# One token load in place of two, key weights in two loads instead of four, and a new order of all work, in a fused attention and GLU kernel

## The chip, the cores and the metric

The kernel runs on one core of one Trainium2 chip. The metric is the device time in microseconds (us). A core has five engines that run at the same time and each work through their own instructions in order: TensorE (PE, matrix products into PSUM), VectorE (DVE), ScalarE (ACT), GpSimd (POOL) and SyncE (SP, which only issues transfers here). They wait for one another through semaphores. Transfers (DMA) are issued by SP or ACT into that engine's own queue and are moved by 16 DMA engines.

## What is computed

Two blocks get the same input x (2048 tokens of 512 values, bf16), and a gate per token mixes them. The other input B_x isn't used.

```python
x = A_x
g = _sigmoid((x * gate_w).sum(-1, keepdims=True))
a = _A_ref(x, A_wq, A_wk, A_wv, A_wo, A_beta)
b = _B_ref(x, B_w_gate, B_w_up, B_w_down)
return g * a + (1 - g) * b
```

Block A is attention with a memory. There are 32 heads of 16 values. The tokens are cut into four segments of 512. Within a segment the attention is causal softmax attention; a matrix M and a vector z per head carry what earlier segments held, and a second result is read from them with q after phi(t) = t + 1 for positive t and exp(t) otherwise. A sigmoid of beta mixes both results per head, and wo projects them. Block B is a gated linear unit: (gelu(x w_gate) * (x w_up)) w_down, with 1792 columns in the middle.

## The kernel before, in words

Everything is held with the contracted axis on the partitions. xT is x transposed, 512 tokens at a time, as four blocks of 128 input columns. For each segment s the kernel makes K, Q and V (`project`, tasks K, Q, V), the scores, exponentials, masks and products with V (`attend`: tasks st, exp, msk, pv), the turns of the results (tp, pvp, ot), the memory's read (nz, nd, ndp) and write (mz, mzacc, zq), the gate and up products of the GLU (G, U, with gelu or gd for the gelu and h for the product), and the outputs (out, wo, with wev and oev for the copies and dma for the store).

A task is one step on one engine, such as four matmuls or one copy. Task names carry the segment, a number, and a letter a or b where a product is made in two halves: U0_4b is the second half of the up product of segment 0, column tile 4. A dense half is two matmuls of 512 columns (line 444), a piece of the output is two or three (line 700), a projection wo is four (line 717). The score group st is four or eight small matmuls (line 595) into one large PSUM area X; exp reads the whole of X on ACT (line 601), and the next st can't begin before that. Other products use four PSUM banks, in turn: whoever takes a bank waits until the copy that reads its former content is done.

**The order is written out.** The string `ORDER` at the end of the file lists every task once. `Sched.schedule` walks it and gives each engine its tasks in that order; each engine then works strictly in its order. A word's digit after the colon is the PSUM bank (or the buffer) that the task takes; the letter is the engine where a task has a choice: `a` is ACT and `d` is DVE. So `xev0_1:d` is a copy made by DVE. `Emitter.plan` adds the waits: a task waits for the writers of what it reads and for the readers of what it overwrites.

**The start.** `ld_w` (line 329) issues a plain load, as task ld_ followed by its name. The first segment's x isn't transposed by the transfer, as that of later segments is (`ld_xt`, line 333), but on PE: four pieces of 128 tokens are loaded as rows into a free buffer (x0_0 to x0_3, 128 KB each), PE transposes them against an identity matrix (`turn_x0`, xtr0_0 to xtr0_3, line 772, four transposes each), and DVE copies each result into xT (xev0_0 to xev0_3, line 780). The key weights come as four blocks of 128 rows (wk0 to wk3, 128 KB each). x0_0, x0_2, wk0, wk2 are in this order in SP's queue, x0_1, x0_3, wk1, wk3 in ACT's; wq (two loads), wv, beta and the gate weights follow in SP's. Two tasks wake0 and wake1 (line 366) multiply constants before anything has arrived.

The first segment's K is made in a special way. K0_k0 to K0_k3 (line 466) each take one block i of the key weights and of xT, and add its share for the first 256 tokens to all four banks; K0_ki needs x pieces 0 and 1 and key block i. K0_0b to K0_3b (line 472) make the other 256 tokens. Kev copies a bank to kT (line 436 on ACT, 437 on DVE), kpada and kpadb make the padded keys on DVE (line 483) that the scores need. Q0 and V0 follow.

**The end.** The last outputs' copies (oev, line 721, DVE) and stores (line 726) follow the last wo matmuls, whose 512 columns are made in two halves for the last two token tiles.

Of the kernel before, what the change touches and what calls it, by code (L numbers as in the profile page):

```python
# [235 lines left out]
def _build(es, nc, A_x, A_wq, A_wk, A_wv, A_wo, A_beta, B_w_gate, B_w_up, B_w_down, gate_w, out):  # L236
# [91 lines left out]
    def ld_w(name, eng, dst, src, writes, size, wait=()):  # L328
        load(name, eng, lambda e: e.dma_start(dst, src), writes, size=size, wait=[("ld", w) for w in wait])
# [544 lines left out]
out0_1_0:2 exp1_0D Kev2_3:d Q2_3b Kev2_0:d out0_1_1 Qev2_3:d out0_1_2 st1_0E:0 out0_1_3 kpadb2_3 exp1_0E pvp0_31
msk1_0B ktr1_2 go0 V2_3a:3 vsh1_01 vsh1_00 V2_3b phqc1_0 ktr1_0 ld_wo20 out0_3_0:0 ot0_2 st1_0C:0 out0_1_4 out0_3_1
Vev2_3:a wev0_1:d phka2_0 exp1_0C G1_11a:3 msk1_0E G1_11b kpadb2_0 K2_2a:1 st1_1A:0 out0_0_0:2 K2_2b out0_0_1 out0_0_2
vsh1_20 ot0_3 gd1_11 phqc1_2 Kev2_2:d msk1_0C out0_0_3 msk1_0D vsh1_21 gelu1 wo0_1_0:1 out0_0_4 ktr1_3 wev0_0:d
out0_3_2 out0_3_3 msk1_0A out0_3_4 oev0_1_0 pv1_0:31 exp1_1A wev0_3:a tp1_d00:1 tp1_d01:2 st1_1B:0 ld_x3_2 wo0_0_0:2
# [5 lines left out]
G2_5a:0 G2_5b Gev2_5:a ndp1_0 tp1_d10:1 G2_0b kpada2_3 G2_3b Gev2_0:d st1_2C:0 gate1:0 exp1_2C msk1_2C kpada2_0
Gev2_3:d mz1 G2_1a:2 G2_1b msk1_2B G2_12a:3 mzacc1 st1_2D:0 G2_12b phkb2_2 gz1 Gev2_1:d kpadb2_1 G2_6a:0 dma0_0 G2_6b
G2_9a:1 pvp1_11 exp1_2D Gev2_6:d wo0_2_0:2 G2_9b gd2_9 G2_8a:0 G2_8b oev0_2_0 ndp1_1 wo0_3_0:2 gd2_12 msk1_2D gd2_8
U1_7a:1 U1_7b gelu2 U1_0a:0 phkc2_0 U1_0b G2_13a:3 G2_13b h1_7 oev0_3_0 pvp1_10 U1_3a:1 gd2_13 h1_0 U1_3b h1_3
st1_2E:0 Q2_0a:2 kpadb2_2 exp1_2E U2_5a:3 U2_5b phqa2_2 Q2_0b ot1_0 V2_0a:1 U1_8a:0 h2_5 V2_0b Vev2_0:d phqb2_2
msk1_2E Qev2_0:d st1_3A:0 U1_5a:3 exp1_3A U1_8b U1_5b h1_8 pv1_2:12 st1_3B:0 tp1_d20:2 K3_1a:0 K3_1b exp1_3B h1_5
U1_1a:1 tp1_d21:1 U1_13a:3 U1_13b pvp1_20 pvp1_21 Kev3_1:a st1_3C:0 ktr2_0 U1_11a:2 K3_0a:0 U1_1b U1_11b exp1_3C zq1  # L890
h1_1 h1_11 K3_0b st1_3D:0 V2_2a:1 h1_13 exp1_3D dma2_0 U1_4a:2 V2_2b Q3_0a:3 U1_4b st2_0A:0 ot1_1 Vev2_2:d h1_4
Kev3_0:d Q3_0b msk1_3B ktr2_1 V2_1a:1 msk1_3C exp2_0A msk1_3A Qev3_0:d msk1_3D V2_1b msk2_0A pv1_3:02 st2_0B:0
# [64 lines left out]
```

## Time and profile before

| what | value |
|---|---|
| median of 3 runs | 266.27 us (266.22 to 266.43) |
| the profiled execution | 265.91 us |
| its span, first to last instruction | 264.2 us |
| matmuls | 2829 |
| DMA queues: packets, share of the 16 engines | SP's queue 23454, 22.1%; ACT's queue 720, 0.7% |
| read from HBM, written | 8.14 MB, 2.10 MB |

The profile is one execution, and its times count from the start of the span. A row of an engine's timeline gives the start, the length and the count of like instructions; in brackets stands how long the engine had been idle and who ended that. Matmuls are pipelined: a 512-column one is shown as 380 ns long, though the next starts earlier, so rows of PE overlap and busy time is not a measure of pace. The chain that ended last is followed back from the last instruction: at each step to what released it, or to the instruction before it on its engine. A granted clock of 1.0 is shown for PE.

### The profile page before, as it was taken

Reading aid. Unit: us, or ns where it says so; the run is one execution under the profiler, and the core shown is the slowest. Engines: PE = TensorE matmul, PEld = TensorE weight load, DVE = VectorE, ACT = ScalarE, POOL = GpSimd, SP = SyncE. Lnnn points to the kernel's source line nnn. Section 1 sums busy time; section 2 is a strip of 40 time slices with the busy share of each in tenths; the row PEclk is TensorE's granted clock in tenths of the full one; section 3 lists DMA queues with packets and bytes.
Section 4 is the critical chain, followed back from the end, with each engine's and each line's share of the span. In section 5 each row is a group of like instructions: output and inputs, shape, how many; then the busy total and the mean of one; then the engine's idle time right before and its main releaser. Section 6 shows DMA issues by size and latency. Waiting matters only on the chain.

```text
span 264.2 us, 6633 instructions
## 1 busy us (share of the span) xinstructions
PE 259.8 (98%) x2829; PEld 113.0 (43%) x2829; DVE 203.0 (77%) x381; ACT 205.8 (78%) x166; POOL 97.6 (37%) x159
## 2 busy tenths in 40 slices
PE   8999999999999999999999999999999999999996
PEld 5633434443344443454434343434344443434443
DVE  2678544698989539989788889889986798977864
ACT  1688899989988998999878887569879967376612
POOL 6017333054434635060273535344525035144500
PEclk9999999999999999999999999999999999999999
DMA  6966169930013230002002000010101000000102
GB/s 205 359 115 180 38 77 209 212 116 2 0 42 78 61 82 0 2 4 60 2 0 65 0 2 2 20 42 11 42 14 43 2 2 0 22 20 2 40 2 79
DMA packets 24203, 14.92 MB, mean 56 GB/s; under 512 B 14574, under 2 KB 23150, under 8 KB 24174
## 3 DMA queue, kind: packets, MB, share of 16 engines
q1 hardware_dynamic: 23454, 13.91, 22.1%
q10 hardware_dynamic: 720, 0.59, 0.7%
q8 instruction: 22, 0.36, 0.6%
q14 instruction: 7, 0.06, 0.1%
HBM read 8.14 MB, written 2.10 MB: 39 GB/s over the span
## 4 chain that ended last, share of the span: by engine, by line
PE 92%; DVE 5%; DMA 1%; issue 1%; SPq 0%
PE psD L444 51%; PE psD L700 17%; PE psX L595 9%; PE psD L638 7%; PE psD L717 5%; DMA wk<-in_A_wk_dram 1%; DVE tT L514 1%; DVE phq L457 1%; DVE gb L687 1%; PE psD L466 1%; PE psD L472 1%; DVE kD L483 1%; PE psX L539 0%; PE psD L563 0%; PE psD L529 0%
## 5 line engine op out<-in xcount | busy, mean ns | idle before, releaser
L601 ACT ACTIVATE pt<-psX 128x2048 bf16<-128x2048 f32 x72 | 135.1, 1877 | 34.1 <-PE psX L595 33.9
L607 POOL TENSOR_TENSOR pt<-pt,ctri 128x256 bf16<-128x256 bf16 x128 | 92.4, 730 | 149.5 <-ACT pt L601 132.4
L444 PE MATMUL psD<-xT,wu 128*128 128x512 bf16 x224 | 56.1, 380 | 0.0
L700 PE MATMUL psD<-wd,gb 128*128 128x512 bf16 x224 | 55.1, 380 | 0.0
L444 PE MATMUL psD<-xT,wg 128*128 128x512 bf16 x224 | 54.6, 380 | 0.3 <-DVE gb L687 0.3
L687 DVE TENSOR_TENSOR gb<-psD,gb 128x512 bf16<-128x512 f32 x56 | 37.5, 683 | 10.1 <-PE psD L444 9.9
L514 DVE STREAM_TRANSPOSE tT<-psD 128x512 f32<-128x512 f32 x35 | 23.8, 701 | 13.3 <-PE psD L638 12.8
L444 PEld LDWEIGHTS psD<-xT,wg 128*128 128x128 bf16 x224 | 20.4, 98 | 26.9 <-issue 2.6
L700 PEld LDWEIGHTS psD<-wd,gb 128*128 128x128 bf16 x224 | 20.2, 98 | 26.0 <-issue 3.7
L444 PEld LDWEIGHTS psD<-xT,wu 128*128 128x128 bf16 x224 | 20.0, 98 | 26.1 <-issue 3.5
L595 PE MATMUL psX<-qT,kD 32*128 32x192 bf16 (+7 forms) x512 | 28.5, 287 | 0.2 <-DVE tT L514 0.2
L595 PEld LDWEIGHTS psX<-qT,kD 32*128 32x128 bf16 x512 | 8.2, 92 | 24.6 <-ACT pt L601 19.0
L638 PE MATMUL psD<-pt,vnat 64*17 64x128 bf16 (+7 forms) x512 | 18.7, 283 | 0.0
L649 DVE SCALAR_TENSOR_TENSOR ob<-tT,gq,rc 128x256 bf16<-128x256 f32 x32 | 17.5, 546 | 1.1
L638 PE MATMUL psD<-pt,vsh 64*17 64x128 bf16 (+7 forms) x512 | 18.3, 283 | 0.0
L444 PE MATMUL psD<-wv,xT 128*128 128x512 bf16 x64 | 17.5, 380 | 0.0
L444 PE MATMUL psD<-xT,wq 128*128 128x512 bf16 x64 | 16.6, 380 | 0.0
L437 DVE CAST gb<-psD 128x512 bf16<-128x512 f32 x20 | 13.6, 682 | 3.9 <-PE psD L444 3.8
L717 PE MATMUL psD<-wo,oT 128*128 128x512 bf16 (+1 forms) x72 | 16.2, 356 | 0.0
L678 ACT ACTIVATE gb<-psD 128x512 bf16<-128x512 f32 x28 | 15.0, 603 | 0.6 <-PE psD L444 0.5
L638 PEld LDWEIGHTS psD<-pt,vnat 64*17 64x17 bf16 x512 | 11.6, 86 | 9.1 <-issue 4.7
L721 DVE SCALAR_TENSOR_TENSOR ost<-psD,gtok,wds 128x512 bf16<-128x512 f32 (+1 forms) x18 | 12.2, 685 | 2.9 <-PE psD L717 2.7
(94 smaller groups left out, 250.6 us busy)
## 6 DMA issues: line engine op xcount, KB each, us to landing
out_dram<-ost SPq DMA_DIRECT2D x15, 128.0 KB, 1.7
wg<-in_B_w_gate_dram SPq DMA_DIRECT2D x2, 896.0 KB, 4.8
wu<-in_B_w_up_dram SPq DMA_DIRECT2D x2, 896.0 KB, 5.4
wd<-in_B_w_down_dram SPq DMA_DIRECT2D x2, 896.0 KB, 8.7
vsh<-vnat SPq DMA_DIRECT2D x16, 68.0 KB, 2.1
wq<-in_A_wq_dram SPq DMA_DIRECT2D x2, 256.0 KB, 4.8
wv<-in_A_wv_dram SPq DMA_DIRECT2D x1, 512.0 KB, 5.4
pt<-in_A_x_dram SPq DMA_DIRECT2D x2, 128.0 KB, 2.5
```

The costliest lines, as they stand in the source:

```text
L437: (DVE, 0.60, [I(lambda e: e.tensor_copy(dst, src()), [bk(sl), *reads], writes)]),
L444: one(f"{name}{'abcd'[h // 2]}", PE, 2 * T_MM, [I(lambda e, i=i: e.matmul(BK[sl.i][:, :], lhs(i), rhs(i), start=(i == 0), stop=(i == n - 1 ...
L514: one(f"tp{name}", DVE, 0.605, [I(lambda e, ts=ts, bank=bank: e.transpose(tT[ts.i][:, :], bank()), [key], [("tT", ts)])])
L595: ins.append(I(lambda e, c=c, kb=kb, ncol=ncol, c0=c0, g=g: e.matmul(XALL[:, g * 512 + c0:g * 512 + c0 + ncol], kD[b][quad(g), c, kb, :], ...
L601: one(f"exp{s}_{name}", ACT, 2048 * 0.000833 + 0.05, [I(lambda e: e.activation(pt[slot][:, :, :], xin, ACTF.Exp, scale=ATT_SCALE), [("X", ...
L607: ins.append(I(lambda e, mv=mv: e.tensor_tensor(mv, mv, cm, ALU.mult), [("pt", slot), ("causal",)], [("pt", slot)]))
L638: ins.append(I(lambda e, kb=kb, slot=slot, c0=c0, n=n, g=g, c=c, r0=r0, sl=banks[j], va=va: e.matmul(BK[sl.i][32 * c:32 * c + 17, 64 * kb: ...
L649: I(lambda e, ts=ts, t=t, j=j, dst=dst: e.scalar_tensor_tensor(out=dst, in0=t_rows(ts, 16), scalar=gq[:, 2 * t + j:2 * t + j + 1], in1=rc_ ...
L678: one(f"gd{s}_{ft}", ACT, 0.485, [I(lambda e, gi=gi, f=f, sl=sl: e.activation(gb[gi][:, f, :], BK[sl.i][:, :], ACTF.Gelu_apprx_tanh), [bk( ...
L687: one(f"h{s}_{ft}", DVE, 0.605, [I(lambda e, sl=sl, gi=gi, f=f: e.tensor_tensor(gb[gi][:, f, :], BK[sl.i][:, :], gb[gi][:, f, :], ALU.mult ...
L700: mm.append(I(lambda e, fb=fb, gi=gi, f=f, q=q, sl=sl: e.matmul(BK[sl.i][:, :], gb[gi][:, f, q], wd[:, fb, :], start=(fb == 0), stop=(fb = ...
L717: one(f"wo{s}_{qt}_{ci}", PE, 4 * T_MM / len(parts), [I(lambda e, kb=kb, q=q, so=so, c=c: e.matmul(BK[so.i][:, c], oT[:, kb, q], wo[:, kb, ...
```

## The change

The last two pieces of x0 become one transfer of 256 KB, x0_2, second in SP's queue; pieces 0 and 1 stay as they are, first in SP's and in ACT's. The key weights become two transfers of 256 KB: wk0 (blocks 0 and 1) second in ACT's queue, wk1 (blocks 2 and 3) third in SP's. What is computed is the same, and so are the buffers. The order of all tasks, the banks and the choice of ACT or DVE for copies are new throughout: two of the four xT copies go to ACT, four more of the scaled copies wev and two more of the copies of gate products.

```diff
-    for q in range(4):
-        ld_w(f"x0_{q}", (SP, ACT)[q % 2], pt[stage[0]][:, q, :], A_x[0, 128 * q:128 * q + 128, :], [("xs", q)], 0.125)
-    for i in range(4):
-        ld_w(f"wk{i}", (SP, ACT)[i % 2], wk[:, i, :], wsrc(A_wk)[:, i, :], [("wk", i)], 0.125)
+    for q, (eng, n) in enumerate(((SP, 1), (ACT, 1), (SP, 2))):
+        ld_w(f"x0_{q}", eng, pt[stage[0]][:, q:q + n, :],
+             A_x[0, 128 * q:128 * (q + n), :].rearrange("(q p) d -> p q d", p=P), [("xs", q + j) for j in range(n)],
+             0.125 * n)
+    for h, eng in enumerate((ACT, SP)):
+        ld_w(f"wk{h}", eng, wk[:, halves[h], :], wsrc(A_wk)[:, halves[h], :], [("wk", 2 * h), ("wk", 2 * h + 1)], 0.25)
```

Of the order, the stretches that the text speaks of. The start:

```diff
-wake0:0 masks causal0 ld_x0_1 ld_x0_0 ld_x0_2 ident xtr0_1 vones0 ld_wk0 ld_x0_3 ld_wk2 wake1 ld_wk1 xtr0_0:0 ld_wq0
-ld_wq1 ld_wk3 xtr0_3 xev0_0:d ld_wv xev0_1:d ld_beta xtr0_2 ld_wg0 K0_k0:2031 xev0_2:d K0_k1 K0_k2 ld_wg1 xev0_3:d
-K0_k3 ld_x1_2 K0_1b Kev0_1:a ld_x1_1 kpada0_1 K0_2b kpadb0_1 K0_0b K0_3b Kev0_2:a Kev0_0:a Kev0_3:d Q0_1a:0 Q0_2a:3
+ld_x0_0 wake0:0 wake1 ld_x0_1 ld_wk0 ident xtr0_0:2 ld_x0_2 ld_wk1 masks ld_wq0 vones0 xev0_0:d xtr0_1 xtr0_3 xtr0_2
+xev0_1:a ld_wq1 K0_k0:3021 ld_wv K0_k1 ld_beta ld_wg0 xev0_3:d xev0_2:a ld_wg1 K0_k2 ld_x1_2 K0_k3 ld_x1_1 K0_3b K0_0b
...
+causal0 Q0_2b Qev0_2:a kpada0_2 Q0_0b kpadb0_0 kpada0_1 phka0_2 Q0_3b Qev0_3:a kpadb0_2 Q0_1a:0 kpadb0_1 Q0_1b
+Qev0_0:d V0_1a:2 V0_3a:1 kpada0_0 causal phkb0_2 Qev0_1:d st0_0A:0 V0_0a:0 phkc0_2 V0_3b G0_3a:3 Vev0_3:d V0_0b V0_1b
```

Around the first memory write:

```diff
-U0_4b phqa1_0 ld_x2_0 phkb1_2 h0_8 st0_2C:0 exp0_2C U0_9a:2 pvp0_11 U0_9b h0_4 gate0:3 msk0_2C h0_9 h0_11 mz0 st0_2D:0
-gz0 mzacc0 kpada1_1 ot0_0 U0_5a:1 U0_5b exp0_2D U0_7a:0 U0_1a:2 kpada1_2 U0_7b st0_2E:0 V1_2a:3 V1_2b h0_7 exp0_2E
-G1_5a:0 ld_x2_3 G1_5b msk0_2B U0_1b Gev1_5:a kpadb1_0 h0_5 st0_3A:0 exp0_3A h0_1 U0_6a:1 U0_6b Vev1_2:d U0_12a:0
+U0_4a:3 st0_2C:0 U0_11a:1 U0_11b Qev1_0:a gate0:0 exp0_2C phka1_0 h0_11 ld_wo21 mz0 st0_2D:0 gz0 U0_4b G1_5a:1 V1_2a:2
+G1_5b exp0_2D V1_2b msk0_2C phka1_2 mzacc0 st0_2E:0 U0_7a:0 Gev1_5:a U0_5a:1 h0_4 U0_1a:3 msk0_2A Vev1_2:d msk0_2D
```

Around gelu2, beside the scores of segment 1 (new order alone), and around the memory read of segment 2:

```diff
+st1_2D:0 msk1_2B Gev2_3:d Gev2_0:d phkb2_2 G2_6b G2_8a:1 wo0_2_0:2 G2_12a:3 exp1_2D Gev2_6:d G2_12b gd2_12 G2_9a:0
+G2_8b zq1 G2_9b oev0_2_0 U1_7a:2 gd2_8 gd2_9 U1_8a:3 phkc2_2 G2_13a:1 U1_7b U1_8b phkc2_0 h1_7 G2_13b wo0_3_0:0
+pvp1_11 msk1_2D oev0_3_0 msk1_2C U1_0a:2 st1_2E:0 U1_0b gelu2 gd2_13 U2_5a:1 Q2_0a:0 U2_5b h1_0 h1_8 exp1_2E V2_0a:2
+Q2_0b kpada2_2 Qev2_0:a U1_3a:3 kpadb2_2 h2_5 pvp1_10 U1_3b msk1_2E st1_3A:0 V2_0b h1_3 U1_5a:1 U1_5b Vev2_0:d
...
-kpadb3_0 pv2_0:20 Vev3_1:a st2_1B:0 h1_10 exp2_1B tp2_d00:2 U1_12a:1 tp2_d01:1 U1_12b out1_0_0:3 out1_0_1 phqc2_2
-phqc2_0 st2_1C:0 V3_3a:0 msk2_1B Q3_2a:2 h1_12 out1_0_2 V3_3b exp2_1C ot1_2 nz2:1 tp2_z:0 st2_1D:0 Q3_2b out1_0_3
+K3_3a:3 out1_0_0:1 K3_3b tp2_d01:2 pvp1_20 phqb2_2 exp2_1B out1_0_1 Kev3_3:a st2_1C:0 tp2_d00:1 msk2_1B U1_12a:0
+out1_0_2 exp2_1C ot1_2 ktr2_2 U1_12b V3_3a:3 V3_3b phqc2_2 st2_1D:0 Q3_2a:2 h1_12 msk2_1C exp2_1D pvp2_00 Q3_2b
+out1_0_3 out1_0_4 Qev3_2:a msk2_1D kpadb3_0 st2_2A:0 nz2:0 exp2_2A wev1_0:d tp2_z:0 Vev3_3:a kpadb3_3 wo1_0_0:2
+oev1_0_0 pv2_1:01 st2_2B:0 out1_1_0:3 out1_1_1 out1_1_2 exp2_2B nzp2 dma3_0 V3_2a:2 st2_2C:0 out1_1_3 exp2_2C go1
...
-wo1_1_0:0 exp2_2C pvp2_10 tp2_d11:1 pvp2_11 V3_2a:3 dma4_0 out1_1_3 nd2:0 nzp2 tp2_m1:0 tp2_m0:1 out1_2_1 out1_1_4
-ndp2_1 V3_2b tp2_m3:2 tp2_m2:0 out1_2_2 Vev3_2:a msk2_2C out1_2_3 wev1_1:a out1_3_0:3 msk2_2B phqa3_2 st2_2D:0 exp2_2D
+pvp2_01 tp2_d11:2 out1_1_4 tp2_d10:1 msk2_2B pvp2_11 pvp2_10 wo1_1_0:1 ktr2_0 nd2:0 V3_2b wev1_1:a out1_3_0:3 Vev3_2:a
+out1_2_0:0 tp2_m0:1 tp2_m3:2 ndp2_0 tp2_m1:0 tp2_m2:1 out1_2_1 msk2_2C out1_3_1 out1_3_2 st2_2D:0 out1_2_2 exp2_2D
```

The end:

```diff
-tp3_d30:2 pvp3_31 out3_1_3 pvp3_30 out3_1_4 out3_2_4 wev3_1:a out3_3_0:1 out3_3_1 ot3_3 wo3_0_0:0 wo3_1_0:3 dma10_0
-oev3_0_0 wev3_2:a out3_3_2 out3_3_3 out3_3_4 dma12_0 oev3_1_0 wo3_2_1:0 wo3_2_0:2 oev3_2_1 oev3_2_0 wo3_3_0:3 wev3_3:a
-dma13_0 dma14_1 oev3_3_0 wo3_3_1:1 oev3_3_1 dma15_0 dma15_1
+out3_2_4 wev3_1:a dma11_0 pvp3_31 out3_3_0:1 pvp3_30 ot3_3 out3_3_1 wo3_0_0:0 oev3_0_0 dma12_0 wo3_1_0:3 out3_3_2
+out3_3_3 out3_3_4 oev3_1_0 wo3_2_1:0 wo3_2_0:3 wev3_2:a wo3_3_0:2 oev3_2_1 oev3_2_0 wo3_3_1:0 wev3_3:a dma13_0
+oev3_3_0 dma14_1 dma15_0 oev3_3_1 dma15_1
```

More of the change, by code (lines that the diff above doesn't have):

```diff
@@ L874 @@
[L874 to L878, printed above, removed]
@@ L884 @@
[L884 to L888, printed above, removed]
@@ L889 @@
[L889 to L892, printed above, removed]
-Vev2_1:a U2_6a:1 tp1_d31:2 U2_6b tp1_d30:1 U1_9a:2 U2_13a:3 h2_6 U1_9b vsh2_01 exp2_0B phqa2_0 msk2_0B st2_0C:0
@@ new lines @@
+out0_1_2 V2_3b phqb1_0 out0_3_1 st1_0C:0 out0_3_2 Vev2_3:d zq0 go0 out0_1_3 msk1_0E G1_11b ot0_2 out0_1_4 exp1_0C
+K2_3a:1 K2_3b wev0_1:d ot0_3 gd1_11 st1_1A:0 out0_0_0:2 msk1_0A wo0_1_0:0 Kev2_3:d out0_3_3 out0_0_1 kpada2_1 phqc1_0
+gelu1 vsh1_20 ktr1_3 vsh1_21 out0_0_2 msk1_0C exp1_1A oev0_1_0 out0_3_4 phka2_0 wev0_3:a ld_x3_2 K2_2a:0 K2_2b
+out0_0_3 out0_0_4 Kev2_2:d pv1_0:10 phka2_2 st1_1B:0 wev0_0:d tp1_d00:1 wo0_0_0:3 exp1_1B Q2_1a:2 Q2_1b Q2_2a:1
+oev0_0_0 st1_1C:0 exp1_1C nz1:3 tp1_d01:0 Qev2_1:d msk1_1C out0_2_0:0 msk1_1B out0_2_1 Q2_2b msk1_1A out0_2_2 st1_1D:0
```

106 lines of the change are left out of this document (55 added, 51 removed).

## The prediction

> **What bounds the kernel now.** I read the page first, then the chain that ended last in order of time, and then only the places where TensorE (PE) was late. The engine table comes first, then pieces of the chain (start, length, what):
>
> ```profile
> span 264.2 us, 6633 instructions
> ...
> PE 259.8 (98%) x2829; PEld 113.0 (43%) x2829; DVE 203.0 (77%) x381; ACT 205.8 (78%) x166; POOL 97.6 (37%) x159
> ```
>
> ```profile
> 1.71 3.77 DMA wk<-in_A_wk_dram
> ...
> 5.62 1.95 PE psD L466 x16
> 7.57 1.75 PE psD L472 x16
> 9.31 4.32 PE psD L444 x20
> ...
> 13.96 2.27 PE psD L444 x10
> 16.22 0.33 PE psX L595 x8
> ...
> 155.66 2.72 DVE phq L457 x2
> ...
> 261.17 0.92 DVE ost L721 x2
> ```
>
> PE is busy for 98% of the span, and DVE and ACT for 77% and 78%. The reader is to see that the chain is a start of 5.62 us that ends in a transfer, then PE almost without a break, then a short tail behind the last matmul. Twenty 512-column matmuls take 4.32 us, so one starts every 0.216 us; ten of them take 2.27 where a small group (scores, L595) follows, which is 0.11 for the switch. A new order can therefore change three things only: when the first K matmul starts (5.62), the waits of PE after it, and the tail. PE's own sum does not move: the matmuls are the same, and counted through both orders PE goes from full matmuls to a small group 76 times in each.
>
> The waits show where a PE row starts later than 0.216 us times the count of the row before it allows (PE's timeline at four places: start, length, what):
>
> ```profile
> 58.74 1.04 PE L444 MATMUL psD<-wv,xT 128*128 128x512 bf16 x4
> 60.11 1.04 PE L444 MATMUL psD<-xT,wg 128*128 128x512 bf16 x4 [0.33 <-DVE gb L687]
> ...
> 158.37 0.59 PE L444 MATMUL psD<-wv,xT 128*128 128x512 bf16 x2
> 159.04 0.39 PE L529 MATMUL psD<-phq,zq 128*8 128x512 bf16 x4
> ...
> 172.29 1.67 PE L700 MATMUL psD<-wd,gb 128*128 128x512 bf16 x7
> 174.18 0.40 PE L595 MATMUL psX<-qT,kD 32*128 32x320 bf16 x8 [0.21 <-DVE tT L514]
> ...
> 209.12 2.11 PE L444 MATMUL psD<-xT,wu 128*128 128x512 bf16 x9
> 211.26 0.39 PE L595 MATMUL psX<-qT,kD 32*128 32x512 bf16 x4
> ```
>
> Four matmuls from 58.74 end their turn at 59.60; the next came at 60.11: about 0.5 late. With 0.11 for the switch the others are late by 159.04 - 158.91 = 0.13, 174.18 - 173.91 = 0.27 and 211.26 - 211.17 = 0.09. Together that is 1.0 us, all that a better order can win behind the start.
>
> **The change part by part: the start.** These are the timeline's rows of the start, then the times from issue to landing (x0 pieces, all four key pieces, the first key piece of ACT's queue), then what the DMA engines moved in each stretch (last figure, GB/s):
>
> ```profile
> 0.80 0.87 SPq L329 DMA_DIRECT2D pt<-in_A_x_dram  x2
> 0.81 0.89 ACTq L329 DMA_DIRECT2D pt<-in_A_x_dram  x2
> 0.84 2.61 PE L366 MATMUL psX<-const-bfloat16-1.0 128*128 128x512 bf16 x8 [0.84 <-PEq L942]
> ...
> 1.71 0.91 SPq L329 DMA_DIRECT2D wk<-in_A_wk_dram  x2
> 1.74 0.94 ACTq L329 DMA_DIRECT2D wk<-in_A_wk_dram  x2
> ...
> 4.26 0.85 PEld L772 LDWEIGHTS psX<-ident,pt 128*128 128x128 bf16 x8
> ...
> 4.91 1.26 DVE L780 COPY xT<-psX 128x512 bf16<-128x512 bf16 x3
> ```
>
> ```profile
> DMA to landing us min/median/max: 2.3/2.6/3.0
> ...
> DMA to landing us min/median/max: 3.8/4.2/4.4
> ...
> DMA to landing us min/median/max: 4.2/4.2/4.2
> ```
>
> ```profile
> 1.80:2.70 0.90, 0.90 (x4) 0.29 (x2) 0.00 (x0) 0.00 (x0) 0.68 (x4) 1.00 0.91 250
> 2.70:3.50 0.80, 0.80 (x7) 0.37 (x5) 0.00 (x0) 0.80 (x1) 0.64 (x5) 1.00 1.03 325
> 3.50:4.50 1.00, 1.00 (x11) 1.00 (x11) 0.00 (x0) 0.49 (x1) 0.76 (x4) 1.00 0.73 213
> 4.50:5.50 1.00, 0.88 (x9) 0.62 (x6) 0.84 (x3) 0.00 (x0) 0.77 (x5) 1.00 0.88 288
> ...
> 6.50:7.50 1.00, 1.00 (x11) 0.90 (x10) 0.00 (x0) 0.00 (x0) 0.00 (x0) 1.00 1.07 374
> ```
>
> Now wk0 is third in SP's queue and lands at 1.71 + 3.77 = 5.48; wk1, third in ACT's, lands at 1.74 + 4.2 = 5.9. K0_k0 starts 0.14 after the first. All transposes of x0 are over by then (the last loads start by 5.1), so they are free today.
>
> In the new order both x0_2 (two pieces, 256 KB, second in SP's queue) and the new wk0 (two blocks, 256 KB, second in ACT's) have 128 KB ahead of them. Each ends when its queue has moved 384 KB, which is just what stands before the end of wk0 and of wk1 today. So no key block comes sooner by its place alone. The cost of x0_2 is bounded below by the two pieces as they are (issued by 1.25, 3.0 at most: 4.2) and above by wk1's landing (5.9). I work out between them: by the stretches 225 kB are moved by 2.7, 485 by 3.5, 698 by 4.5, and the 786 kB of both queues by 4.8. Landings come behind such sums: the last x0 piece is due at 3.7 by them and lands at 4.2, wk0 is due at 4.8 and lands at 5.48, so 0.6. That gives 5.4; with 325 GB/s kept from 2.7 on, as half as many transfers may allow, 4.4 + 0.6 = 5.0. I take 5.2. For wk0 I take 5.6, between 5.48 and 5.9.
>
> Behind x0_2 stand, on PE's queue, xtr0_3 and xtr0_2, and K0_k0 stands behind them. Eight transposes take 0.85 (the row of 4.26), so they now lie on the path: 5.2 + 0.05 + 0.85 = 6.1, past wk0 and past the two evictions that K0_k0 reads (xev0_0 on DVE and xev0_1 now on ACT, side by side, 0.42 each by the row of 4.91). K0 starts 0.48 later. The second key transfer, third in SP's queue, brings the sum to 1049 kB: by the last stretches 5.7, landed 6.3, and its first reader comes at 6.1 + 0.87: hidden. Today's first sixteen K matmuls take 1.95 and the next 1.75, 0.109 each; of the 0.2, about 0.16 is one matmul's own passage and 0.04 is left for waits on landings, which now go. So the start costs **+0.44**. The wq transfers are next in SP's queue, 0.7 each at 374 GB/s, so in by 8.0, and the first Q matmul comes at 9.6; fewer issues on ACT cost nothing, as ACT has no work before the evictions.
>
> The Trainium skill, "DMA: Bandwidth & Descriptors", Queues, rings and completion order, says that an engine takes turns between the queues that it has work for. That is the rule that speaks against the change, and the row of 3.50 agrees as far as it can: both queues were then moving, at 213 GB/s together. The same page (Bandwidth) says that larger transfers come nearer to the peak; by it x0_2 would land near 4.7 and the start cost nothing, and the 374 GB/s at 6.5, with 256 KB transfers, speaks for it.
>
> **The waits.** These rows price them (ACT's groups, the table loads among them; DVE's products; the padded keys, ns min/median/max):
>
> ```profile
> L601 ACT ACTIVATE pt<-psX 128x2048 bf16<-128x2048 f32 x72 | 135.1, 1877 | 34.1 <-PE psX L595 33.9
> L678 ACT ACTIVATE gb<-psD 128x512 bf16<-128x512 f32 x28 | 15.0, 603 | 0.6 <-PE psD L444 0.5
> L675 ACT ACTIVATE gb<-gb 128x3584 bf16<-128x3584 bf16 x4 | 12.8, 3195 | 0.0
> L678 ACT ACT_TABLE_LOAD x5 | 6.4, 1283 | 0.1
> ```
>
> ```profile
> L687 DVE TENSOR_TENSOR gb<-psD,gb 128x512 bf16<-128x512 f32 x56 | 37.5, 683 | 10.1 <-PE psD L444 9.9
> ```
>
> ```profile
> L483 DVE TENSOR_SCALAR kD<-kT,maskA x16: 307/345/819, 8.7 to 183.8; 128x512 bf16<-128x512 bf16 x16
> ```
>
> - 60.11 (G1_5a waits for h0_7): goes, **-0.5**. Today G1_5a takes h0_7's bank, behind gz0, mzacc0, two padded keys and ot0_0 on DVE. The new G1_5a takes h0_11's bank, and h0_11 stands ahead of gz0. Late next is U0_7a, behind gz0 and mzacc0: some 2.7 us of DVE against 3.5 of PE, so it holds.
> - 159.04 (nz2 waits for h1_12): goes, **-0.13**. Today two phqc pieces (2.72) stand ahead of h1_12; now one does, and from U1_12b's end to nz2 PE has 3.9 us against 1.36 + 0.68.
> - 174.18 (st2_2D behind four turns and ndp2): stays. The same five DVE operations and the same sixteen matmuls stand between nd2 and st2_2D.
> - 211.26 (st3_1A behind gelu3): stays, with the same ACT work.
> - New: st1_3A. From st1_2D to st1_3A PE has 52 full matmuls, two score groups and two switches: 11.2 + 0.66 + 0.22 = 12.1. ACT has the scores' 0.45, two exponentials, two table loads, four single gelus (about 0.55 each in a row) and the long one: 0.45 + 3.75 + 2.57 + 2.2 + 3.2 = 12.2. **+0.14**.
> - Three more places have under 0.1 us to spare: st0_0A behind Qev0_1 (six matmuls and a switch, 1.40, against 0.60 + 0.04 + 0.68 + 0.14), wo0_1_0 behind gd1_11, and pv2_1 behind tp2_z. Each costs from 0 to 0.48, the spread of the padded keys (0.82 against 0.345); I take 0.1 each, **+0.3**.
>
> Eight evictions more go to ACT (four scaled copies, two gate, two x0), about 5 us on an engine with 58 us to spare; hidden by PE. The tail is the same: seventeen full matmuls cover the last turns in both, and the last four projections stand alike, so **0**.
>
> Sum: 0.44 - 0.5 - 0.13 + 0.14 + 0.3 = +0.25. The profiled execution took 265.91 us in all (1.7 around its span); it would take 266.16. The median of the runs is 266.27, 0.36 above the profiled one; with the same step, 266.5.
>
> **The rivals.** A measurement of this kernel can tell about 0.2% (0.5 us) from no change.
>
> - Slower, x0_2 lands late. At the upper bound, 5.9, K0 starts at 6.8 and the start costs 1.15: 267.2. It decides from a landing at 5.5 on, where the sum passes 0.5. For it: the slow stretch at 3.5 lies in x0_2's time, and the unchanged rates alone give 5.4. Against: fewer, larger transfers.
> - Slower, new waits. If the three tight places each cost 0.48, and one more as the 60.11 wait did appears, 1.9 takes the place of my 0.3: 268.1. For it: every evicting choice and the slots are new. Against: ACT and DVE are no fuller.
> - Slower, the clock. The eight wake matmuls (2944 columns in 2.61, 0.89 ns each) run at half the pace of K0 (256 columns in 0.109, 0.43), so PE quickens between. PE will now be idle about 0.8 us before the last transposes; if it quickens that much later or more, half of K0 at the slow pace is +1.7: 268.2. The Trainium skill, "TensorE: Matmul & The Clock Gate", Part 1, says that the clock rises after a busy window of about 3.4 us; no run here shows yet what a gap does.
> - Faster. x0_2 lands by 4.7, as the fuller rate allows, wk0 by 5.5 and the start costs nothing; the tight places hold, and of the old waits only that of ACT stays: -0.9 + 0.14 = -0.75, 265.5. For it: the two largest waits are of accidents of order. Against: a new order has its own.
>
> **How the numbers follow.** Forecast (within 0.2%) 0.38; faster 0.27; late x0_2 0.15, new waits 0.15, clock 0.05, together slower 0.35. The forecast's own range is 266.1 to 266.8. To hold 8 in 10, the range takes in the faster case and the late x0_2 and leaves out the far ends of faster, new waits and clock: 265.3 to 267.6.
>
> **What would show it.** In the profile after: the landing of the pt transfer of 256 KB (5.2), the first matmul of K0 (6.1) with two groups of transposes just before it, no wait of wg behind the products near 60, waits at the scores near 127, 174 and 211. The prediction fails if the key matmuls start by 5.6, or if waits of over 0.3 us stand where I saw none.

## The result, and the profile after

The changed kernel takes 265.28 us (median of 6 runs, 265.08 to 265.74), the kernel before on the same chip 266.31 (265.89 to 266.51). The ratio is 0.9954, with a 95% interval of 0.9932 to 0.9976: about 1.0 us faster, where +0.2 was forecast, and just under the stated range of 265.3 to 267.6. The profiled execution took 265.16 us against 265.91 before, so 0.75 us are there to be found in the two traces; that of before is the fastest of its six, so they show less than the medians do. Some executions of most kernels here last about 2 us longer, and since the medians and ratios take them in, the table below has a second median without those that lie more than 1.5 us above the fastest of their kernel.

The page's first lines of after (the span; the engines):

```profile
span 263.4 us, 6630 instructions
...
PE 259.6 (99%) x2829; PEld 113.4 (43%) x2829; DVE 200.3 (76%) x373; ACT 210.7 (80%) x174; POOL 96.4 (37%) x159
```

ACT is busy for 4.9 us more than before and DVE for 2.7 less, since copies changed engines; PE's sum is as it was. The start, first in the chain that ended last (start, length, what), then as PE's rows:

```profile
1.25 3.56 DMA pt<-in_A_x_dram
5.72 1.91 PE psD L468 x16
7.63 1.75 PE psD L474 x16
9.37 4.32 PE psD L446 x20
```

```profile
4.86 0.86 PE L774 MATMUL psX<-ident,pt 128*128 128x128 bf16 x8 [0.33 <-DMA pt<-in_A_x_dram]
5.56 2.07 PE L468 MATMUL psD<-xT,wk 128*128 128x256 bf16 x16
7.46 1.91 PE L474 MATMUL psD<-xT,wk 128*128 128x256 bf16 x16
9.21 3.62 PE L446 MATMUL psD<-xT,wq 128*128 128x512 bf16 x16
12.66 1.03 PE L446 MATMUL psD<-wv,xT 128*128 128x512 bf16 x4
13.62 0.39 PE L597 MATMUL psX<-qT,kD 32*128 32x512 bf16 x4
```

The chain now starts with x0_2, as forecast, but x0_2 lands at 1.25 + 3.56 = 4.81, not at 5.2. The eight transposes behind it take 5.56 - 4.86 = 0.70, and K0 starts at 5.56, where it was 5.62 before and 6.1 in the forecast. K0_k2 then waits 0.15 for the second key transfer; the first scores come at 13.62, 0.06 later than before (13.56). Why x0_2 came early shows in the transfers (GB/s is the last figure):

```profile
2.70:3.50 0.80, 0.80 (x7) 0.37 (x4) 0.00 (x0) 0.31 (x1) 0.61 (x4) 1.00 0.91 315
3.50:4.50 1.00, 1.00 (x9) 0.76 (x8) 0.36 (x1) 0.00 (x0) 0.76 (x5) 1.00 1.06 369
4.50:5.50 1.00, 0.67 (x8) 0.64 (x8) 0.07 (x1) 0.60 (x1) 0.94 (x5) 1.00 0.96 323
```

From 3.5 to 4.5 the transfers moved 369 GB/s where they moved 213 before.

From the first scores (st0_0A) to the start of the last projection (wo3_3_1) the time fell from 247.41 us (13.56 to 260.97) to 246.60 (13.62 to 260.22). All that the change won between these two executions, 0.81 us, was won here. PE's rows at the places that the forecast spoke of, each with the row that leads up to it:

```profile
55.83 0.60 PE L446 MATMUL psD<-xT,wu 128*128 128x512 bf16 x2
56.27 0.59 PE L446 MATMUL psD<-xT,wg 128*128 128x512 bf16 x2
...
125.74 1.03 PE L446 MATMUL psD<-xT,wu 128*128 128x512 bf16 x4
126.70 0.39 PE L597 MATMUL psX<-qT,kD 32*128 32x512 bf16 x4
...
161.57 0.39 PE L597 MATMUL psX<-qT,kD 32*128 32x512 bf16 x4
161.89 0.39 PE L531 MATMUL psD<-phq,zq 128*8 128x512 bf16 x4
...
171.16 2.32 PE L702 MATMUL psD<-wd,gb 128*128 128x512 bf16 x10
173.41 0.40 PE L597 MATMUL psX<-qT,kD 32*128 32x320 bf16 x8
...
207.71 3.19 PE L446 MATMUL psD<-xT,wu 128*128 128x512 bf16 x14
210.92 0.39 PE L597 MATMUL psX<-qT,kD 32*128 32x512 bf16 x4
```

With 0.216 us for a 512-column matmul and 0.11 for the switch, G1_5a (56.27, the one that came at 60.11 before), st1_3A (126.70) and st2_2D (173.41: ten matmuls from 171.16 end their turn at 173.43) are on time, and nz2 follows its scores directly. Only st3_1A is late, by 210.92 - 207.71 - 14 x 0.216 - 0.11 = 0.08, as before. So the waits at 60.11, 159.04 and 174.18 are gone, and the new one at st1_3A did not come. The one at 174.18 should have stayed.

### The profile page after: what moved, and what is told of

The parts are those of the page before. It is cut to its first block, busy times and chain, and to the rows that moved or that the text cites. A ratio compares the mean times of both kernels' runs of the same rounds, so it can differ in the third digit from the quotient of the medians.

```text
span 263.4 us, 6630 instructions
## 1 busy us (share of the span) xinstructions
PE 259.6 (99%) x2829; PEld 113.4 (43%) x2829; DVE 200.3 (76%) x373; ACT 210.7 (80%) x174; POOL 96.4 (37%) x159
## 4 chain that ended last, share of the span: by engine, by line
PE 97%; DMA 1%; DVE 0%; SPq 0%; issue 0%
PE psD L446 53%; PE psD L702 19%; PE psX L597 9%; PE psD L640 7%; PE psD L719 5%; DMA pt<-in_A_x_dram 1%; PE psD L468 1%; PE psD L474 1%; PE psD L565 1%; PE psD L415 0%; PE psX L541 0%; PE psD L531 0%; DVE ost L723 0%; PE psX L774 0%; SPq L329 0%
## 5 line engine op out<-in xcount | busy, mean ns | idle before, releaser
L609 POOL TENSOR_TENSOR pt<-pt,ctri 128x256 bf16<-128x256 bf16 x128 | 91.2, 720 | 152.0 <-ACT pt L603 147.6
L446 PE MATMUL psD<-xT,wu 128*128 128x512 bf16 x224 | 56.7, 380 | 0.0
L723 DVE SCALAR_TENSOR_TENSOR ost<-psD,gtok,wds 128x512 bf16<-128x512 f32 (+1 forms) x18 | 12.2, 686 | 6.2 <-PE psD L719 6.1
L439 DVE CAST gb<-psD 128x512 bf16<-128x512 f32 x18 | 11.9, 681 | 4.0 <-PE psD L446 4.0
```

Of the source, the lines that this page charges most:

```text
L446: one(f"{name}{'abcd'[h // 2]}", PE, 2 * T_MM, [I(lambda e, i=i: e.matmul(BK[sl.i][:, :], lhs(i), rhs(i), start=(i == 0), stop=(i == n - 1 ...
L609: ins.append(I(lambda e, mv=mv: e.tensor_tensor(mv, mv, cm, ALU.mult), [("pt", slot), ("causal",)], [("pt", slot)]))
L723: lambda e, so=so, gt=gt, wi=wi, oi=oi, c=c: e.scalar_tensor_tensor(out=ost[oi][:, c], in0=BK[so.i][:, c], scalar=gtok[:, gt:gt + 1], in1= ...
```

## The experiments

The experiments ran on three chips, and each ratio is to the kernel before on the same chip. The second median leaves out the long executions (in brackets how many of how many are left) and has its distance from before's second median on that chip (266.28 to 266.55). PE's instructions are matched one by one with those of before or after, because some of these traces lack some of the 2829 matmul records. "First scores" is the start of st0_0A, "stretch" the time from there to the start of wo3_3_1.

| kernel | median us | second median, from before | ratio to before (95%) | first scores | stretch |
|---|---|---|---|---|---|
| before | 266.31 | 266.31 (6 of 6) | 1 | 13.56 | 247.41 |
| after | 265.28 | 265.28 (6 of 6), -1.03 | 0.9954 (0.9932 to 0.9976) | 13.62 | 246.60 |
| after again | 265.30 | 265.12 (10 of 12), -1.17 | 0.9950 (0.9922 to 0.9978) | 13.38 | 246.76 |
| old order, new loads | 266.26 | 266.26 (12 of 12), -0.17 | 0.9979 (0.9960 to 0.9998) | 14.05 | 247.41 |
| new order, old loads | 265.66 | 265.57 (10 of 12), -0.86 | 0.9977 (0.9957 to 0.9998) | 14.12 | 246.59 |
| padded keys later | 265.86 | 265.86 (12 of 12), -0.57 | 0.9967 (0.9947 to 0.9987) | 13.96 | 246.92 |
| masks A, B, C | 266.40 | 266.35 (10 of 12), -0.08 | 1.0001 (0.9982 to 1.0020) | 14.12 | 247.38 |
| padded keys later, masks B, C, A | 265.49 | 265.48 (11 of 12), -0.80 | 0.9966 (0.9945 to 0.9987) | 15.92 | 246.63 |
| after, masks C, B, A | 265.23 | 265.15 (10 of 12), -1.13 | 0.9961 (0.9935 to 0.9987) | 13.85 | 246.65 |
| after, masks C, A, B | 265.49 | 265.40 (11 of 12), -1.15 | 0.9956 (0.9931 to 0.9981) | 13.67 | 246.98 |
| after, small loads | 267.51 | 265.67 (5 of 12), -0.61 | 1.0021 (0.9990 to 1.0052) | 14.08 | 246.66 |
| after, short wake | 266.68 | 266.68 (10 of 10), +0.13 | 0.9982 (0.9956 to 1.0008) | 14.94 | 246.59 |

In kernels that differ at the start alone the stretch repeats to a few hundredths of a us (246.59 to 246.66, once 246.76), so a wait of 0.3 us shows plainly. In the times it doesn't: their intervals reach 0.5 us to either side.

**Which half of the change won.** The theory was that the order won everything; the rival gave the loads a part. First the new loads (as in the diff above) in the order of before, from which only the issues of the merged pieces go:

```diff
-wake0:0 masks causal0 ld_x0_1 ld_x0_0 ld_x0_2 ident xtr0_1 vones0 ld_wk0 ld_x0_3 ld_wk2 wake1 ld_wk1 xtr0_0:0 ld_wq0
-ld_wq1 ld_wk3 xtr0_3 xev0_0:d ld_wv xev0_1:d ld_beta xtr0_2 ld_wg0 K0_k0:2031 xev0_2:d K0_k1 K0_k2 ld_wg1 xev0_3:d
+wake0:0 masks causal0 ld_x0_1 ld_x0_0 ld_x0_2 ident xtr0_1 vones0 ld_wk0 wake1 ld_wk1 xtr0_0:0 ld_wq0
+ld_wq1 xtr0_3 xev0_0:d ld_wv xev0_1:d ld_beta xtr0_2 ld_wg0 K0_k0:2031 xev0_2:d K0_k1 K0_k2 ld_wg1 xev0_3:d
```

> The kernel before with the new loads alone (x0_2 of 256 KB, two key transfers), its own order kept. Theory A (the loads are worth nothing, the gain is in the order's waits): x0_2 lands near 4.8 and the first key transfer near 5.1, the second near 6.5, so the first Q matmul stays at 9.15 to 9.25, the waits of 0.49, 0.28 and 0.1 us at 60, 174 and 211 stay, and the time is that of before within 0.1 us (ratio 1.000). Rival B (the loads bring the gain): 0.5 to 1.0 us faster than before, ratio 0.996 to 0.998.

Then the new order with the eight old loads:

```diff
-ld_x0_0 wake0:0 wake1 ld_x0_1 ld_wk0 ident xtr0_0:2 ld_x0_2 ld_wk1 masks ld_wq0 vones0 xev0_0:d xtr0_1 xtr0_3 xtr0_2
+ld_x0_0 wake0:0 wake1 ld_x0_1 ld_x0_2 ld_x0_3 ld_wk0 ident xtr0_0:2 ld_wk1 ld_wk2 ld_wk3 masks ld_wq0 vones0 xev0_0:d xtr0_1 xtr0_3 xtr0_2
```

> The changed kernel's order with the old loads (four pieces of x0, four key blocks, queues as before). Theory A: the first Q matmul comes near 9.15, everything behind it as in the changed kernel, so 0.75 to 1.0 us faster than before (ratio 0.996 to 0.997). Rival B: the time goes back to that of before, ratio 1.000.

The stretch decides for the waits: 247.41 with the new loads alone, to the hundredth that of before, and 246.59 with the new order alone, that of after. The loads act on the start only, and there both expectations were too early: the first Q matmul comes at 9.85 and 9.93, where about 9.2 was expected, and the first scores at 14.05 and 14.12.

The trace of before is the odd one among those with the old loads. Its first key block landed at 5.48 and K0 started at 5.62; in the four others (the new order with the old loads, and the three kernels with small edits of the old order) the block lands at 5.70 to 6.08 and K0 starts at 5.83 to 6.22. The new loads alone start K0 at 5.88, no better. With both new (after twice, the two kernels that change only masks, and the short wake at the end of this section) it starts at 5.29 to 5.73, and with the full wake the first scores come at 13.38 to 13.85; in every other trace but that of before they come at 13.96 or later. So the two halves together start the kernel some tenths sooner than the two profiled executions show. The second medians say the same: 0.17 below before with the loads alone, 0.86 with the order alone, 1.03 to 1.17 with both. The interval of the loads alone ends at 0.9998, but long executions are 5 of the 35 of before behind it and none of the 12 of this kernel; I don't build on that.

The changed kernel itself, on the second chip, came out as the rival had it: first scores at 13.38 and not near 14.1, and 265.30, 0.36 below the new order with the old loads on the first chip.

> The changed kernel itself, to stand on the same chip as the next three. Theory A (the new order of the work is the gain, the loads are worth nothing): its start is like that of the kernel with the new order and the old loads (first scores st0_0A at about 14.1 us here), the stretch from st0_0A to the last wo3_3_1 takes 246.6 us, and the time is within 0.3 us of 265.66. Rival B (the new loads bring a part): the time is 0.3 to 0.5 us below 265.66.

**The wait at 60.11.** In the trace of before the two padded keys ahead of h0_7 take 0.75 and 0.82 us, where the median of their line is 0.345; GpSimd is masking all the while (DVE's rows, then POOL's):

```profile
57.33 0.75 DVE L483 TENSOR_SCALAR kD<-kT,maskA 128x512 bf16<-128x512 bf16 x1
58.01 0.70 DVE L657 STREAM_TRANSPOSE oT<-ob 128x512 bf16<-128x512 bf16 x1
58.63 0.82 DVE L483 TENSOR_SCALAR kD<-kT,maskA 128x512 bf16<-128x512 bf16 x1
59.37 0.68 DVE L687 TENSOR_TENSOR gb<-psD,gb 128x512 bf16<-128x512 f32 x1
```

```profile
55.84 4.20 POOL L607 TENSOR_TENSOR pt<-pt,ctri 128x256 bf16<-128x256 bf16 x6 [13.82 <-ACT pt L601]
```

The experiment puts both behind h0_7:

```diff
-gz0 mzacc0 kpada1_1 ot0_0 U0_5a:1 U0_5b exp0_2D U0_7a:0 U0_1a:2 kpada1_2 U0_7b st0_2E:0 V1_2a:3 V1_2b h0_7 exp0_2E
+gz0 mzacc0 ot0_0 U0_5a:1 U0_5b exp0_2D U0_7a:0 U0_1a:2 U0_7b st0_2E:0 V1_2a:3 V1_2b h0_7 kpada1_1 kpada1_2 exp0_2E
```

> The kernel before, with DVE's two padded keys kpada1_1 and kpada1_2 moved behind h0_7 and nothing else. If the wait of 0.49 us at 60.11 lies on the path and comes from DVE's order, the first gate matmul after V1_2b starts near 59.65 in place of 60.11, and the kernel is 0.4 to 0.5 us faster (ratio 0.998). Rival: PE has slack later and the end does not move, ratio 1.000.

PE's rows at that place, in this kernel:

```profile
59.14 1.04 PE L444 MATMUL psD<-wv,xT 128*128 128x512 bf16 x4
60.01 1.03 PE L444 MATMUL psD<-xT,wg 128*128 128x512 bf16 x4
```

The next four matmuls follow after 0.87 us, on time; the stretch is 247.41 - 246.92 = 0.49 shorter and the time 0.6 lower. The price of the forecast's first step was right. Beside the masks the two keys took 0.88 us longer than their median together, more than the wait; but this run moves the keys and not the masks, so the masks' part in the wait is worked out, not shown.

**The wait at 174.18.** Between the forecast's "same five DVE operations" and the trace stood GpSimd again. Each row here is one instruction of before; ndp2_1 (line 548) takes 1.06 us, where its like in after (ndp2_0, line 550) takes 0.65:

```profile
171.69 0.66 POOL L607 TENSOR_TENSOR pt<-pt,ctri 128x256 bf16<-128x256 bf16 x1
...
172.31 1.12 POOL L607 TENSOR_TENSOR pt<-pt,ctri 128x256 bf16<-128x256 bf16 x1
...
171.84 1.06 DVE L548 TENSOR_TENSOR omem<-tT,rcm 128x512 bf16<-128x512 f32 x1
```

```profile
171.35 0.65 DVE L550 TENSOR_TENSOR omem<-tT,rcm 128x512 bf16<-128x512 f32 x1
```

In after the mask before it has ended (five masks ended at 171.34, since two ran early, from 166.70). The first test moved only masks, in the order of before, to A, B, C at the place of C:

```diff
-ndp2_1 V3_2b tp2_m3:2 tp2_m2:0 out1_2_2 Vev3_2:a msk2_2C out1_2_3 wev1_1:a out1_3_0:3 msk2_2B phqa3_2 st2_2D:0 exp2_2D
-kpada3_0 out1_2_4 out1_3_1 kpada3_3 U2_11a:2 U2_11b oev1_1_0 kpadb3_3 h2_11 st2_2E:0 exp2_2E msk2_2A wo1_2_0:0
+ndp2_1 V3_2b tp2_m3:2 tp2_m2:0 out1_2_2 Vev3_2:a msk2_2A msk2_2B msk2_2C out1_2_3 wev1_1:a out1_3_0:3 phqa3_2 st2_2D:0 exp2_2D
+kpada3_0 out1_2_4 out1_3_1 kpada3_3 U2_11a:2 U2_11b oev1_1_0 kpadb3_3 h2_11 st2_2E:0 exp2_2E wo1_2_0:0
```

> The kernel before, with POOL's masks of segment 2 in the order 2A, 2B, 2C in place of 2C, 2B, 2A, so that POOL is done by about 171 when DVE comes to ndp2_1; DVE's and PE's orders are untouched. Theory C (DVE's product is slowed by POOL's work at the same time): ndp2_1 takes 0.65 to 0.70 us in place of 1.06, the score group st2_2D starts without its wait of 0.28, and the kernel is 0.25 us faster (ratio 0.999). Rival D (my prediction's reading: the wait is the sum of five DVE operations of fixed length): ndp2_1 and the wait stay as they are, ratio 1.000.

ndp2_1 took 0.65, st2_2D was on time, and yet the time stayed. The stretch shows why: up to st2_2C it was 0.25 longer than before, from st2_2C to st2_2D 0.28 shorter. Mask A had met another instruction of VectorE, in a place where PE waited for the next copy on that engine (L649 takes 0.48 elsewhere):

```profile
164.88 0.97 DVE L649 SCALAR_TENSOR_TENSOR ob<-tT,gq,rc 128x256 bf16<-128x256 f32 x1
```

```profile
164.90 0.67 POOL L607 TENSOR_TENSOR pt<-pt,ctri 128x256 bf16<-128x256 bf16 x1 [1.18 <-ACT pt L601]
```

The collision had moved, with about the same price (here VectorE was the slower one though it began 0.03 earlier; the last section comes back to that). So the next kernel took the order B, C, A, which was to meet neither, together with the later padded keys. Against the masks A, B, C:

```diff
-... Vev3_2:a msk2_2A msk2_2B msk2_2C out1_2_3 wev1_1:a ...
+... Vev3_2:a msk2_2B msk2_2C msk2_2A out1_2_3 wev1_1:a ...
```

> The kernel before with two small edits of its order: the two padded keys behind h0_7, and GpSimd's masks of sample 2 in the order B, C, A at the place of C. Theory A (the two waits are the collisions of GpSimd with VectorE, and this order of the masks meets no two-operand instruction of VectorE): ndp2_1 takes 0.65 us, st0_0A to wo3_3_1 takes 246.65 (247.41 less 0.49 and 0.28), and the time is 0.75 us below the kernel before, as good as the whole new order. Rival B (the collision only moves, as it did with the masks in the order A, B, C): the stretch takes 246.9 and the time is 0.5 us below, no better than with the padded keys alone.

The stretch is 246.63, as theory A had it (246.65), and within 0.03 of the changed kernel's 246.60. Four moved words of the old order do to the stretch what the new order of everything does. Against the padded keys later alone, only the masks differ, and the stretch is 0.29 shorter: the masks alone made the wait at 174.18. The median is 0.9 below before, the second median 0.8. The expectation was wrong in one point: a mask does meet a two-operand instruction here too (at 169.90 an L649 takes 0.85 us instead of 0.48), but no score group comes later for it. (The first scores came late in this trace, at 15.92; the last section has why.)

**Which of the two engines pays.** The next kernel puts mask B back behind C in the changed kernel, so that GpSimd masks from 169.58 to 173.43 as it did before.

```diff
-pvp2_01 tp2_d11:2 out1_1_4 tp2_d10:1 msk2_2B pvp2_11 pvp2_10 wo1_1_0:1 ktr2_0 nd2:0 V3_2b wev1_1:a out1_3_0:3 Vev3_2:a
-out1_2_0:0 tp2_m0:1 tp2_m3:2 ndp2_0 tp2_m1:0 tp2_m2:1 out1_2_1 msk2_2C out1_3_1 out1_3_2 st2_2D:0 out1_2_2 exp2_2D
+pvp2_01 tp2_d11:2 out1_1_4 tp2_d10:1 pvp2_11 pvp2_10 wo1_1_0:1 ktr2_0 nd2:0 V3_2b wev1_1:a out1_3_0:3 Vev3_2:a
+out1_2_0:0 tp2_m0:1 tp2_m3:2 ndp2_0 tp2_m1:0 tp2_m2:1 out1_2_1 msk2_2C msk2_2B out1_3_1 out1_3_2 st2_2D:0 out1_2_2 exp2_2D
```

> The changed kernel with GpSimd's masks of sample 2 back in the order C, B, A. Theory A (masks beside VectorE's multiplication of the memory output make it 1.06 instead of 0.65 us, and that made st2_2D late): ndp2_0 takes 1.0 to 1.1 us, st2_2D comes 0.25 to 0.30 us later against its neighbours, and the time is 0.2 to 0.3 us above that of the changed kernel. Rival B (the multiplication is not in the way of st2_2D in this order): ndp2_0 slows, st2_2D stays, and the time is within 0.1.

My theory missed: no slower ndp2_0, no later st2_2D, no other time. The rows, DVE's, POOL's and PE's:

```profile
171.63 0.65 DVE L550 TENSOR_TENSOR omem<-tT,rcm 128x512 bf16<-128x512 f32 x1
```

```profile
171.70 1.11 POOL L609 TENSOR_TENSOR pt<-pt,ctri 128x256 bf16<-128x256 bf16 x1
```

```profile
171.23 2.54 PE L702 MATMUL psD<-wd,gb 128*128 128x512 bf16 x11
173.70 0.40 PE L597 MATMUL psX<-qT,kD 32*128 32x320 bf16 x8
```

Here it is the mask that takes 1.11 instead of 0.67. ndp2_0 began 0.07 us ahead of it; in before the mask had begun 0.15 ahead of ndp2_1. So the theory became: the one that begins first runs at its own length, and the other waits until it ends. The order C, A, B has no pause between masks at that moment, and tests it (against C, B, A):

```diff
-... tp2_m2:1 out1_2_1 msk2_2C msk2_2B out1_3_1 out1_3_2 ...
-oev1_1_0 out1_2_3 dma4_0 out1_2_4 ndp2_1 U2_11a:1 msk2_2A st2_2E:0 kpada3_3 U2_11b phqa3_2 wev1_2:a h2_11 msk2_2D
+... tp2_m2:1 out1_2_1 msk2_2C msk2_2A msk2_2B out1_3_1 out1_3_2 ...
+oev1_1_0 out1_2_3 dma4_0 out1_2_4 ndp2_1 U2_11a:1 st2_2E:0 kpada3_3 U2_11b phqa3_2 wev1_2:a h2_11 msk2_2D
```

> The changed kernel with GpSimd's masks of sample 2 in the order C, A, B. With the order C, B, A VectorE's multiplication ndp2_0 began at 171.630, in the 79 ns between the end of one mask at 171.620 and the begin of the next at 171.699, and took 0.65 us, while that mask took 1.11. In the order C, A, B the mask that runs at that moment should begin some 50 ns ahead of the multiplication. Theory A (the one that begins first holds the memory, the other waits for its end): ndp2_0 takes 1.1 to 1.2 us, the mask its 0.67, st2_2D comes 0.25 to 0.40 later against st2_2C than the 6.52 us of the changed kernel, and the time is 0.25 to 0.4 above that of the changed kernel (265.15 on this scale). Rival B (the slowing hangs on something else than which begins first): ndp2_0 0.65 again, or slow without a later st2_2D, and no change of the time within 0.1.

```profile
171.34 0.67 POOL L609 TENSOR_TENSOR pt<-pt,ctri 128x256 bf16<-128x256 bf16 x1
```

```profile
171.39 1.17 DVE L550 TENSOR_TENSOR omem<-tT,rcm 128x512 bf16<-128x512 f32 x1
```

```profile
171.20 2.32 PE L702 MATMUL psD<-wd,gb 128*128 128x512 bf16 x10
173.84 0.40 PE L597 MATMUL psX<-qT,kD 32*128 32x320 bf16 x8 [0.32 <-DVE tT L516]
```

The mask began 0.05 us ahead, and now it keeps its 0.67 and VectorE takes 1.17. PE's wait is back, with the releaser that it had at 174.18 before. From st2_2C to st2_2D it is 6.91 us instead of 6.52, and the stretch is 0.38 longer than the changed kernel's. The expected rise of the time did not show: the second medians of C, B, A and C, A, B lie 1.13 and 1.15 below before's, on two chips.

**The start.** Two experiments on the changed kernel. The first cuts each transfer of 256 KB in two, with the same bytes in the same queues (x0_0, x0_2, x0_3, wk2, wk3 in SP's; x0_1, wk0, wk1 in ACT's):

```diff
+    for q, eng in enumerate((SP, ACT, SP, SP)):
+        ld_w(f"x0_{q}", eng, pt[stage[0]][:, q, :], A_x[0, 128 * q:128 * q + 128, :], [("xs", q)], 0.125)
+    for i, eng in enumerate((ACT, ACT, SP, SP)):
+        ld_w(f"wk{i}", eng, wk[:, i, :], wsrc(A_wk)[:, i, :], [("wk", i)], 0.125)
```

> The changed kernel with the same bytes on the same queues, but each transfer of 256 KB cut in two of 128 KB. Theory A (the size of a transfer is what let the queue move 369 GB/s in place of 213 there): x0_3 lands 0.4 to 0.6 us later than in the changed kernel and the first scores start 0.3 to 0.5 us later. Rival B (it is the place in the queues, not the size): landings and start as in the changed kernel within 0.1, and the time too.

The last x piece, the chain's first transfer and what PE did behind it:

```profile
1.71 3.96 DMA pt<-in_A_x_dram
```

```profile
5.72 0.62 PE L772 MATMUL psX<-ident,pt 128*128 128x128 bf16 x8 [1.12 <-DMA pt<-in_A_x_dram]
```

x0_3 lands at 5.67, 0.86 after the changed kernel's x0_2, and the first scores come at 14.08, 0.2 to 0.7 later than in the four traces with the large transfers. The landing itself is clearer than the scores: x0_2 landed at 4.66 to 4.96 in those four. So the size has a part in it. But my reason for it was wrong: all of x and the key weights, 1 MB, had landed by 6.45 here and by 6.53 in after, so small transfers did not slow the sum. The landings fit another reading, which no run isolates: x0_2 and wk0 came sooner here (4.16 and 4.39), and the four pieces behind them came close together (x0_3 5.67, wk1 5.86, wk2 6.07, wk3 6.45), as if moved at the same time. The slow stretch isn't tied to small transfers either: from 3.5 to 4.5 this kernel moved 302 GB/s, and the new order with the old loads 343. The forecast's reading by the Trainium skill, "DMA: Bandwidth & Descriptors", Bandwidth, that larger transfers come nearer to the peak, had the landing nearly right (4.7, and 4.81 measured); these sums of bytes do not show that reason. The second median is 0.5 above that of the changed kernel on the same chip, but from 5 of 12 executions.

An earlier x0_2 alone would bring little more, by one trace. With the masks C, A, B it landed at 4.66, the earliest, and K0 started at 5.29; but K0_k2 then waited 0.47 for the second key transfer, which landed at 6.58.

The second cuts the constant matmuls at the start from eight (2944 columns) to one of 128, which computes nothing that is used:

```diff
-    for i, cols in enumerate(([512] * 5 + [128] * 3, [128] * 1)):
+    for i, cols in enumerate(([128] * 1, [128] * 1)):
```

> The changed kernel with its first group of matmuls on a constant cut from eight to one of 128 columns, so that TensorE does nothing from about 1 us to the first transposes at 3.5 us. Nothing that is computed hangs on these matmuls. Theory A (TensorE's pace doubles only after a time of work, and the constant matmuls supply that time): the 16 matmuls of the first key groups take about 3.6 us instead of 2.0, the first scores start 1.5 to 2.2 us later, and the time is 1.5 to 2.2 us above that of the changed kernel. Rival B (the pace doubles at a set moment near 5.4 us whatever ran before): no change within 0.2.

```profile
5.65 3.29 PE L468 MATMUL psD<-xT,wk 128*128 128x256 bf16 x16
8.78 1.91 PE L474 MATMUL psD<-xT,wk 128*128 128x256 bf16 x16
```

The first sixteen key matmuls are 213 ns apart, up to about 8.5 us, and the others 109. The first scores come at 14.94, 1.1 to 1.6 us later than in the four traces with the full wake: theory A, at a price somewhat under the 1.5 to 2.2 expected. The time follows: the second median is 0.13 above before's, where that of C, A, B on the same chip is 1.15 below.

No experiment points to a version that beats the changed kernel.

## Why the prediction was wrong, point by point

The forecast's sum was +0.25; the two profiled executions differ by -0.75 and the medians by -1.03. By its steps:

- **The start, +0.44.** Measured +0.06 in the two profiled executions, and that is partly the luck of before's, whose K0 started sooner than in four other traces with the old loads; against those the start is a gain of some tenths. The step that failed is "I take 5.2" for x0_2: it landed at 4.81 (4.66 to 5.00 in the six traces with this transfer), because I carried the slow stretch of 213 GB/s over to transfers that moved at 369. My own estimates had held 5.0 and 4.7. The other half of the step was to take before's landing of 5.48 as fixed, where the same transfer lands up to 0.6 later in other traces. The next step, eight transposes for 0.85, was also too dear: 0.70, because the last of them ran 56 ns apart instead of 107. And of K0's "0.04 left for waits on landings, which now go", the reverse came: K0_k2 waits 0.15 for the second key transfer, which I had called hidden.
- **60.11, -0.5.** Right: the wait is gone, and the single edit that removes it is worth 0.49.
- **159.04, -0.13.** Right by the trace; it had no run of its own.
- **174.18, "stays".** Wrong by 0.28, and the step that failed is "the same five DVE operations and the same sixteen matmuls stand between": I counted instructions and took their lengths as fixed. The row of 1.06 us for ndp2_1 beside GpSimd's masks was in the trace, and I had used just this spread (0.345 to 0.82) to price other places.
- **211.26, "stays".** Right: 0.09 before, 0.08 after.
- **st1_3A, +0.14.** Wrong; nothing. From st1_2D (114.60) ACT's chain ended at 126.58, so it took 11.98 and not 12.2: four single gelus and the long one, counted at 5.4 us, took 5.15 in a row. Added up without rounding, the forecast's own terms give 0.06 and not 0.14; either is more than a difference of two sums of 12 us can tell.
- **Three tight places, +0.3.** About 0.1: wo0_1_0 came 0.06 late, pv2_1 by 0.03 at most, st0_0A not at all.
- **The tail, 0.** Right: behind the start of wo3_3_1 stand 264.2 - 260.97 = 3.2 us before and 263.4 - 260.22 = 3.2 after.

With the sizes measured in the two traces: 0.06 - 0.49 - 0.13 - 0.28 + 0.10 = -0.74, against -0.75. Of the rivals the fourth, "faster", held: x0_2 landed at 4.81 where it asked for 4.7, the start cost next to nothing and of the old waits only ACT's stayed. Its "accidents of order" have a name, GpSimd's masks, at 174.18, and by their lengths at 60.11 too. The rival of new waits didn't come. The rival of the clock has a mechanism that the short wake shows, at 1.1 to 1.6 us, but neither profiled execution of the changed kernel meets it.

What stays open is how much the new loads are worth under the new order. K0 starts at 5.29 to 5.73 with them and at 6.17 and 6.22 with small transfers in that order; the first scores come at 13.38 to 13.85 against 14.08 and 14.12. A few tenths are likely, but these are few traces on several chips.

## What to carry to other kernels

Where PE is busy 98% of the time, look at the few places where it is late, and for each at whether the instruction ahead of it had its usual length; a row that is longer than its group's median can name a second engine to look at. Moving the other engine's work out of the way was worth as much as ordering everything anew, but only once it met no other instruction that PE waits for. And the first transfers of a kernel are better priced from several traces than from one stretch's rate in one of them: the same first key block landed anywhere from 5.48 to 6.08 here.
